# Windowed attention with sink keys, then a gated two-layer product: adjacent score blocks, a third bank in the first product, and constant products on TensorE in the first group

## The chip, the core and the metric

The kernel runs on one core of a Trainium2 chip. A core has five engines with instruction queues of their own: TensorE (PE, matrix products and transposes, weight loads shown apart as PEld), VectorE (DVE), ScalarE (ACT), GpSimd (POOL) and SyncE (SP, which issues DMAs here). PE writes to PSUM, which has eight banks of 2 KB in each of 128 partitions; DVE and ACT read PSUM, POOL and the DMA engines do not. The metric is the device time of one execution in microseconds, as the median of several runs.

## The reference

Inputs are `q`, `k`, `v` of shape (4, 8, 768, 64), and two weight matrices of 512 x 2048 and 2048 x 512.

```python
scores = scale * np.matmul(q, k.transpose(0, 1, 3, 2))
keep = is_sink | in_window                  # 4 first keys, or the last 128
scores = np.where(keep, scores, -1000000000.0)
scores = scores - np.max(scores, axis=-1, keepdims=True)
a = np.exp(scores)
a = a / (np.sum(a, axis=-1, keepdims=True) + 1e-09)
attn = np.matmul(a, v)
x = attn.transpose(0, 2, 1, 3).reshape(B * S, H * D)      # 3072 x 512
h = x @ w_in
g = h * (1.0 / (1.0 + np.exp(-1.702 * h)))
out = g @ w_out
```

## The kernel before

The 3072 rows are cut into 12 groups of 256 (`g`, 0 to 11), three for each batch entry. A group goes through attention, then the first product with its activation, then the second product, and three groups are in work at a time: in stage `n` PE does attention of group `n`, the first product of group `n - 1` and the second product of group `n - 2`. The whole order of instructions is written out by hand (`tc.manual_schedule()`), so each engine runs its instructions in the order in which the code issues them, and a wait on one engine holds up all that stands behind it on that engine.

Attention of a group is done for four pairs of heads (`hp`, 0 to 3):

- `qk_block` (L146) transposes q and k on PE into a PSUM tile `tqk`, which DVE or ACT copies to `qkT`. It is used for groups 0 to 3; from group 4 on a DMA transposes (`transposed_qk`, L167).
- `sinks` (L188) gives the four sink scores (`sk`) and, on DVE, their minimum.
- `scores` (L209) gives a pair of heads' scores: eight products of 64 rows each, into a tile `nat` of two banks. Products with `masked_l` and `masked_r`, two constant matrices of 128 x 128, stand in for the keys before the first row.
- `maxima` (L234) is DVE's work on `nat`: a predicated copy, a maximum over rows, and `bias`.
- `weights` (L249) is ACT's: four exponentials from `nat` to `A`.
- `weights_transposed` (L261) transposes `A` to `AT`, on PE and through a PSUM tile `tA` for groups 0 to 2, by DMA from group 3 on. POOL (`upper`, L311) and DVE (`lower`, L301) mask `AT`.
- `values` (L324) multiplies with `v` into a tile `av`, and `normal` (L355) divides on DVE into `xn`. `x_transposed` (L366) turns `xn` into `xT`, on PE for groups 0 and 1 (`tx`), then by DMA.

`hidden` (L384) is the first product, in eight tiles `hT` of two times 128 columns of `w_in`; each tile is 8 products of 128 x 256, and ACT's activation (L397) takes it to `gT`. `out_part` (L403) is a quarter of the second product for 128 rows: four products of 128 x 512 into the tile `o`. `out_store` (L431) copies `o` to `osb` (ACT for the first 128 rows, DVE for the second) and issues the store on SP.

PSUM is split by three tags. `mm` has two banks (`mm_bank`, L103) for `o` and `hT` and, in the first groups, for some of the transposes. `av` has two banks (`av_bank`, L106) for `sk`, `tAs`, `av` and the rest. `nat` has two tiles of two banks. A tile of a tag takes the place of the one two before it of the same tag, and its first product waits until that one has been read.

The order around the change:

- The first group: L479 to L484 transpose group 0's q and k as they land, L504 to L565 are the attention of groups 0 and 1, interleaved, with the loads of weights and later groups on POOL's queue in between. From L568 on `hidden(0, ...)` runs.
- `second` (L630) is the first half of stage `n` from 3 on: the weights of the first two pairs on ACT, the second product of group `n - 2` on PE, with `scores(n, 2)` (L640) between its two halves of 128 rows and `scores(n, 3)` (L648) after the first quarter of the second half. DVE's `maxima` follow each.
- The second half of the stage (L685 to L707) is `hidden(n - 1, F2)` for `F2` from 0 to 7, and between the tiles the sinks and the first two pairs' scores of group `n + 1` (`F2` = 1) and the values of group `n` (`F2` = 3, 4, 6, 7).

Of the kernel before, what the change touches and what calls it, by code (L numbers as in the profile page):

```python
# [10 lines left out]
FP32 = mybir.dt.float32  # L11
FP16 = mybir.dt.float16
# [5 lines left out]
P = 128  # L18
# [39 lines left out]
def kernel(  # L58
# [11 lines left out]
    nc = tc.nc  # L70
# [6 lines left out]
    NF = DF // P  # L77
    NT = S // TG
    NG = B * NT
# [6 lines left out]
    psp = ctx.enter_context(tc.tile_pool(name="psum", bufs=1, space=bass.MemoryType.PSUM))  # L86
# [19 lines left out]
    def av_bank(name, shape, dt=FP32):  # L106
        return psp.tile(list(shape), dt, tag="av", bufs=2, name=name)

    G = [dict() for _ in range(NG)]

    def load_part(g: int, part: int):


        b, t = divmod(g, NT)
        e, i = divmod(part, 2)
        rows = slice(t * TG + i * P, t * TG + (i + 1) * P)
        if part == 0:
            G[g]["qkn"] = work.tile([P, 4, DM], FP16, tag="qkn", bufs=3, name=f"qkn{g}")
        if part < 4:
            dst = G[g]["qkn"][:, part].rearrange("s (h d) -> s h d", h=H)  # L120
        else:
            dst = vn[b][t][:, i, :, 0:D]
        nc.gpsimd.dma_start(dst, (q, k, v)[e][b, :, rows].rearrange("h s d -> s h d"))  # L123
# [22 lines left out]
    def qk_block(g: int, a: int, eng):  # L146

        n, T = G[g]["qkn"], qk_tile(g)
        bank = mm_bank if g == 1 or (g, a // 2) == (0, 0) else av_bank
        tp = bank(f"tqk{g}_{a}", (P, HP, P), FP16)  # L150
        for c in range(HP):
            nc.tensor.transpose(tp[:, c], n[:, a, bass.ts(c, P)], ident)
        eng(out=T[:, bass.ts(a, HP)], in_=tp)  # L153
# [17 lines left out]
    def sink_keys(b: int, copy):  # L171
        kT = G[b * NT]["qkT"]
        for h in range(2):
            copy(
                out=kd[b][bass.ts(h, D), :, bass.ts(h, n_sink)],
                in_=kT[bass.ts(h, D), 1, 0, :, 0:n_sink],
            )

    def sink_values(b: int):
        nc.vector.tensor_tensor(  # L180
            out=vs[b][0:64, :, 0:D],
            in0=vsr[:, b].unsqueeze(1).broadcast_to((64, 16, D)),
            in1=sink_rows[0:64].unsqueeze(2).broadcast_to((64, 16, D)),
            op=ALU.mult,
        )
# [23 lines left out]
    def scores(g: int, hp: int):  # L209

        b, t = divmod(g, NT)
        qkT = G[g]["qkT"]
        nat = psp.tile([P, 2, 2, 2 * P], FP32, tag="nat", bufs=2, name=f"nat{g}_{hp}")
        for i in range(2):
            I = 2 * t + i
            prev = None if I == 0 else qkT[:, 1, 0, hp] if i else G[g - 1]["qkT"][:, 1, 1, hp]
            for part, keys in ((0, prev), (1, qkT[:, 1, i, hp])):
                for h in range(2):
                    r = bass.ts(h, D)
                    o = nat[:, h, i, bass.ts(part, P)]  # L220
                    if keys is None:
                        nc.tensor.matmul(o, masked_l[r], masked_r[r], start=True, stop=True)
                    else:
                        nc.tensor.matmul(o, qkT[r, 0, i, hp], keys[r], start=True, stop=True)  # L224
        G[g]["nat", hp] = nat
# [32 lines left out]
                )  # L258
        G[g]["A", hp] = A

    def weights_transposed(g: int, hp: int):  # L261
        A = G[g]["A", hp]
        AT = work.tile([P, 2, 2, P], FP16, tag="AT", bufs=6, name=f"AT{g}_{hp}")
        flat = AT.rearrange("p h i s -> p (h i) s")
        if g < 3:
            bank = av_bank if g == 2 or (g, hp) == (1, 3) else mm_bank
            tp = bank(f"tA{g}_{hp}", (P, 4, P), FP16)
            for a in range(4):
                nc.tensor.transpose(tp[:, a], A[:, a], ident)
            if g == 0 or hp < (2 if g == 2 else 3):  # L270
                nc.scalar.copy(flat, tp)
            else:
                nc.vector.tensor_copy(out=flat, in_=tp)
        else:
            nc.sync.dma_start_transpose(flat, A.rearrange("p a c -> p (a c)"))
        G[g]["AT", hp] = AT
# [89 lines left out]
    def x_transposed(g: int):  # L366
        xT = work.tile([P, 2 * HP, P], FP16, tag="xT", bufs=3, name=f"xT{g}")
        xn = G[g]["xn"].rearrange("p i a h d -> p (i a h d)")
        if g < 2:
            bank = mm_bank if g == 0 else av_bank  # L370
            for i in range(2):
                tp = bank(f"tx{g}_{i}", (P, HP, P), FP16)
                for c in range(HP):
                    nc.tensor.transpose(tp[:, c], xn[:, (HP * i + c) * P : (HP * i + c + 1) * P], ident)
                if g == 0 or i == 0:
                    nc.scalar.copy(xT[:, bass.ts(i, HP)], tp)
                else:
                    nc.vector.tensor_copy(out=xT[:, bass.ts(i, HP)], in_=tp)
        else:
            nc.sync.dma_start_transpose(xT, xn)  # L380
        G[g]["xT"] = xT.rearrange("p (i c) s -> p i c s", i=2)


    def hidden(g: int, F2: int):  # L384
        xT = G[g]["xT"]
        if F2 == 0:
            G[g]["gT"] = work.tile([P, NF, TG], FP16, tag="gT", bufs=3, name=f"gT{g}")

        bank = av_bank if g == NG - 2 and F2 in (2, 3) else mm_bank
        hT = bank(f"hT{g}_{F2}", (P, 2, 2, P))  # L390
        for f in range(2):
            F = 2 * F2 + f
            for c in range(4):
                nc.tensor.matmul(  # L394
                    hT[:, f], w_in16[:, c, bass.ts(F, P)], xT[:, :, c], start=(c == 0), stop=(c == 3)
                )
        nc.scalar.activation(  # L397
            out=G[g]["gT"][:, 2 * F2 : 2 * F2 + 2].rearrange("p f s -> p (f s)"),
            in_=hT.rearrange("p f i s -> p (f i s)"),
            func=AF.Gelu_apprx_sigmoid,  # L400
        )

    def out_part(g: int, i: int, part: int):  # L403

        if part == 0:
            G[g]["o", i] = mm_bank(f"o{g}_{i}")
        o, gT = G[g]["o", i], G[g]["gT"]
        for F in range(4 * part, 4 * part + 4):
            nc.tensor.matmul(o, gT[:, F, bass.ts(i, P)], w_out16[:, F], start=(F == 0), stop=(F == NF - 1))  # L409

    def out_last(g: int, i: int):
# [30 lines left out]
    ident = constant(nc.sync, "ident", np.eye(P, dtype=np.float16), FP16)  # L442
# [33 lines left out]
    load_w_in(3)  # L476
    for part in range(3):
        load_part(2, part)
    qk_block(0, 0, by_dve)  # L479
    qk_block(0, 1, by_act)  # L480
    sink_values(0)
    qk_block(0, 2, by_dve)
    qk_block(0, 3, by_act)
    sink_keys(0, nc.vector.tensor_copy)  # L484

    def ahead(n: int, hp: int):

        if n < NG:
            if hp == 0:
                sinks(n)  # L490
            scores(n, hp)
            maxima(n, hp)

    def o(g: int, i: int, *parts):
        if 0 <= g < NG:
            for p in parts:
                out_part(g, i, p)

    def valued(g: int, hp: int):
        values(g, hp)  # L500
# [5 lines left out]
    qk_block(1, 0, by_act)  # L506
    weights(0, 0)
    qk_block(1, 1, by_act)
    scores(0, 2)
    maxima(0, 2)  # L510
    weights(0, 1)
    qk_block(1, 2, by_act)
    qk_block(1, 3, by_act)
    scores(0, 3)
    maxima(0, 3)
    sink_terms(0)
# [3 lines left out]
    weights_transposed(0, 1)  # L520
    upper(0, 1)
    load_part(2, 3)
    ahead(1, 0)
    weights(0, 3)
    weights_transposed(0, 2)
    upper(0, 2)
    sink_weights(0)
    lower(0, 0)
# [8 lines left out]
    lower(0, 2)  # L537
    lower(0, 3)
    weights(1, 0)
    weights_transposed(1, 0)  # L540
    scores(1, 2)
    valued(0, 0)
    valued(0, 1)
    weights(1, 1)
    weights_transposed(1, 1)
    upper(1, 0)
    maxima(1, 2)
    scores(1, 3)
# [81 lines left out]
    def second(n: int, g2: int, att: bool):  # L630

        if att and n + 1 < NG and (n + 1) % NT == 0:
            sink_keys((n + 1) // NT, nc.gpsimd.tensor_copy)
        if att:
            for hp in (0, 1):
                weights(n, hp)
                weights_transposed(n, hp)
        o(g2, 0, 0, 1, 2, 3)
        if att:
            scores(n, 2)  # L640
            maxima(n, 2)
        if g2 == NG - 1:
            out_store(g2, 0)
            out_last(g2, 1)
            return
        o(g2, 1, 0)
        if att:
            scores(n, 3)  # L648
            maxima(n, 3)
            sink_terms(n)  # L650
        o(g2, 1, 1, 2, 3)
        out_store(g2, 0)
        if att:
            weights(n, 2)
            weights_transposed(n, 2)
        out_store(g2, 1)
        if att:
            weights(n, 3)
            weights_transposed(n, 3)
            sink_weights(n)  # L660
            lower(n, 0)
            if n + 2 < NG:
                transposed_qk(n + 2)
# [82 lines left out]
```

## Time and profile before

| | |
|---|---|
| three runs, median | 242.43 us |
| lowest, highest | 241.89, 242.43 us |
| the profiled execution | 242.06 us |
| its span, first to last instruction | 240.3 us |
| mean granted TensorE clock over the span, as recorded | 0.993 |
| chain of waits that ended last: PE, DMA, DVE, ACT | 64%, 16%, 7%, 5% |
| `hT` products (L394): 768, mean | 275 ns |
| `o` products (L409): 368, mean | 380 ns |
| activation of one `hT` tile (L397, ACT): mean | 597 ns |
| predicated copy and maximum of one `nat` tile (L236, L240, DVE): mean | 693 and 691 ns |

The busy time of a matrix product in this profile runs from its start to the modelled end of its result, so that products one after another overlap: a group of several shows the time from its first start to its last end. How fast PE really goes is read from the distance between starts. The granted clock is recorded from the first change on.

### The profile page before, as it was taken

What the parts mean: (1) busy time and instruction counts of PE and PEld (TensorE: products, weight loads), DVE (VectorE), ACT (ScalarE), POOL (GpSimd) and SP (SyncE); (2) the same over time, 40 slices, a digit from 0 to 9 for tenths busy, and PEclk for the clock granted to TensorE, in tenths of its full rate; (3) what the DMA queues carried; (4) which work ended last, traced back from release to release, by engine and by line L of the source; (5) the groups of instructions that cost most, each with busy time, mean ns of one, the idle gap of its engine ahead of it and who ended that gap; (6) DMA issues with size and microseconds to landing.
All of it is one profiled execution on the core that took longest, in us unless ns stands there. A gap on an engine that the chain in (4) does not pass through costs nothing.

```text
span 240.3 us, 5810 instructions
## 1 busy us (share of the span) xinstructions
PE 222.3 (93%) x2220; PEld 155.6 (65%) x2220; DVE 147.3 (61%) x388; ACT 156.7 (65%) x356; POOL 103.5 (43%) x158
## 2 busy tenths in 40 slices
PE   1677799999999999999999999999999999999994
PEld 0454578569569469478487486585585685684863
DVE  4787947579478377477675585776692883840100
ACT  2297774884875775785776777667668658760531
POOL 8988484857237357257046057148020310310000
PEclk9999989999999999999999999999999999999999
DMA  9999999999999969989989999999982513503102
GB/s 81 148 193 193 176 207 178 154 142 148 115 154 193 137 157 172 134 158 160 151 142 153 156 165 133 172 138 125 138 196 54 148 21 65 152 5 87 46 0 87
DMA packets 130699, 32.07 MB, mean 133 GB/s; under 512 B 123120, under 2 KB 127728, under 8 KB 130672
## 3 DMA queue, kind: packets, MB, share of 16 engines
q0 software_dynamic: 79104, 13.64, 79.2%
q1 hardware_dynamic: 50992, 17.88, 41.3%
q8 instruction: 17, 0.28, 0.5%
q10 hardware_dynamic: 576, 0.20, 0.3%
q14 instruction: 10, 0.08, 0.1%
HBM read 27.50 MB, written 6.29 MB: 141 GB/s over the span
## 4 chain that ended last, share of the span: by engine, by line
PE 64%; DMA 16%; DVE 7%; ACT 5%; POOL 4%; issue 2%; SPq 1%; ACTq 0%; DVEq 0%; POOLq 0%
PE hT L394 28%; PE o L409 25%; DMA qkn<-in_k_dram 5%; DMA AT<-A 4%; DMA qkT<-qkn 4%; DMA w_in<-in_moe_w_in_dram 3%; POOL qkn L123 3%; DVE m L240 3%; DVE nat L236 3%; PE nat L224 2%; PE av L344 2%; ACT L397 2%; PE av L332 2%; PE av L340 2%; PE o L420 1%
## 5 line engine op out<-in xcount | busy, mean ns | idle before, releaser
L394 PE MATMUL hT<-xT,w_in 128*128 128x256 f16 x768 | 95.6, 275 | 1.4 <-ACT gT L397 0.9
L409 PE MATMUL o<-w_out,gT 128*128 128x512 f16 x368 | 85.3, 380 | 0.0
L397 ACT ACTIVATE gT<-hT 128x512 f16<-128x512 f32 x96 | 56.2, 597 | 41.2 <-PE hT L394 40.9
L394 PEld LDWEIGHTS <-w_in 128*128 128x128 f16 x768 | 72.8, 98 | 13.7 <-issue 1.1
L318 POOL TENSOR_SCALAR_AFFINE_SELECT up<-AT 128x512 f16<-128x512 f16 (+1 forms) x48 | 27.2, 574 | 93.6 <-DMA AT<-A 86.0
L255 ACT ACTIVATE A<-nat,bias 128x128 f16<-128x128 f32 x192 | 53.7, 375 | 18.9 <-DVE bias L244 17.3
L409 PEld LDWEIGHTS <-gT 128*128 128x128 f16 x368 | 33.6, 98 | 37.2
L236 DVE COPY_PREDICATED nat<-prev,nat 128x512 f32<-128x512 uint16 x48 | 33.3, 693 | 28.0 <-PE nat L224 17.9
L240 DVE TENSOR_REDUCE m<-nat 128x4 f32<-128x512 f32 x48 | 33.2, 691 | 1.6
L123 POOL DMA_DIRECT2D vn<-in_v_dram x24 | 21.3, 895 | 5.3 <-DMA w_out<-in_moe_w_out_dram 4.0
L123 POOL DMA_DIRECT2D qkn<-in_q_dram x24 | 21.6, 908 | 1.4 <-POOLq L727 0.8
L123 POOL DMA_DIRECT2D qkn<-in_k_dram x24 | 21.3, 893 | 2.2 <-DMA w_in<-in_moe_w_in_dram 1.7
L362 DVE TENSOR_TENSOR xn<-av,rcp 128x256 f16<-128x256 f32 x48 | 20.4, 425 | 1.7
L305 DVE TENSOR_TENSOR lo<-AT,own 128x512 f16<-128x512 f16 (+1 forms) x48 | 18.7, 412 | 2.3 <-DMA AT<-A 2.3
L340 PE MATMUL av<-vn,up 128*128 128x65 f16 x160 | 18.3, 195 | 0.0
L344 PE MATMUL av<-vn,lo 128*128 128x65 f16 x160 | 18.3, 196 | 0.0
L361 DVE RECIPROCAL rcp<-av 128x4 f32<-128x4 f32 x48 | 8.6, 179 | 14.6 <-PE av L344 14.5
L332 PE MATMUL av<-vs,AsT 128*128 128x130 f16 x80 | 16.5, 224 | 0.5 <-DVE qkT L153 0.3
L224 PEld LDWEIGHTS <-qkT 64*128 64x128 f16 x352 | 11.7, 100 | 7.4 <-issue 6.6
L224 PE MATMUL nat<-qkT 64*128 64x128 f16 x288 | 16.5, 232 | 0.0
L340 PEld LDWEIGHTS <-up 128*128 128x128 f16 x160 | 14.8, 100 | 1.2 <-issue 0.4
L397 ACT ACT_TABLE_LOAD x11 | 14.1, 1283 | 0.2
(58 smaller groups left out, 179.3 us busy)
## 6 DMA issues: line engine op xcount, KB each, us to landing
out_dram<-osb SPq DMA_DIRECT2D x23, 256.0 KB
qkn<-in_q_dram POOLq DMA_DIRECT2D x24, 128.0 KB, 5.6
qkn<-in_k_dram POOLq DMA_DIRECT2D x24, 128.0 KB, 5.5
vn<-in_v_dram POOLq DMA_DIRECT2D x24, 128.0 KB, 6.2
w_in<-in_moe_w_in_dram POOLq DMA_DIRECT2D x4, 512.0 KB, 9.9
w_out<-in_moe_w_out_dram POOLq DMA_DIRECT2D x4, 512.0 KB, 12.4
AT<-A SPq DMA_TRANSPOSE x36
xT<-xn SPq DMA_TRANSPOSE x10
```

The costliest lines, as they stand in the source:

```text
L123: nc.gpsimd.dma_start(dst, (q, k, v)[e][b, :, rows].rearrange("h s d -> s h d"))
L224: nc.tensor.matmul(o, qkT[r, 0, i, hp], keys[r], start=True, stop=True)
L236: nc.vector.copy_predicated(out=nat[:, :, :, P:], mask=kinds(take_prev, g % NT), data=nat[:, :, :, 0:P])
L240: nc.vector.tensor_reduce(out=m1.rearrange("p h i -> p (h i)"), in_=nat.rearrange("p h i c -> p (h i) c")[:, :, P:], axis=AX.X, op=ALU.max,)
L255: nc.scalar.activation(out=A[:, 2 * h + i], in_=nat[:, h, i, P:], func=AF.Exp, bias=bias[:, i, hp, h : h + 1], scale=scale,)
L318: nc.gpsimd.affine_select(out=out, in_=in_, pattern=[[0, rows], [-1, P]], compare_op=ALU.is_gt, fill=zero_reg, base=0, channel_multiplier=1,)
L332: nc.tensor.matmul(av[:, i].rearrange("p h d -> p (h d)"), AsT, vs[b][:, c : c + 2].rearrange("p h d -> p (h d)"), start=True, stop=False,)
L340: nc.tensor.matmul(av[:, i, h], up[:, h, i], vn[b][J // 2][:, J % 2, head], start=False, stop=False)
L344: nc.tensor.matmul(av[:, i, h], own_w[:, h, i], vn[b][t][:, i, head], start=(I == 0), stop=(I == 0 or h == 1))
L394: nc.tensor.matmul(hT[:, f], w_in16[:, c, bass.ts(F, P)], xT[:, :, c], start=(c == 0), stop=(c == 3))
L397: nc.scalar.activation(out=G[g]["gT"][:, 2 * F2 : 2 * F2 + 2].rearrange("p f s -> p (f s)"), in_=hT.rearrange("p f i s -> p (f i s)"), fun ...
L409: nc.tensor.matmul(o, gT[:, F, bass.ts(i, P)], w_out16[:, F], start=(F == 0), stop=(F == NF - 1))
```

## The change

Three things are changed.

`second` now issues two products of the second half (`out_part(g2, 1, 0, 2)`), then `scores(n, 2)` and `scores(n, 3)` one right after the other, then both `maxima`, then the remaining fourteen products. `out_part` takes a range of products for this in place of a quarter.

`hidden` takes a bank of tag `av` in place of `mm` for the tile `F2` = 2 of groups 2 to 9. For group 10 it took one for `F2` = 2 and 3 before, and still does.

A new function `busy(n, out)` issues `n` products on PE whose result nothing reads: products of `masked_l` and `masked_r`, or, where `out` is of 16 bits, transposes of the identity. It is called thirteen times in the first two groups, for 151 products in all: 34 before the first transposes, 12, 7, 6 and 3 after each of group 0's `qk_block`, 24 and 8 ahead of `scores(0, 2)` and `scores(0, 3)`, 6 ahead of `scores(1, 0)`, 14 ahead of `scores(1, 1)`, 16 and 6 ahead of the transposes of `A` in `weights_transposed(1, 0)` and `(1, 1)`, and 10 and 5 within the first tile of `x_transposed(0)`. They write to a tile `warm0` of tag `nat`, a tile `warm1` of tag `av`, or to the place that the transpose after them writes.

```diff
+    def busy(n: int, out):
+        for _ in range(n):
+            if out.dtype == FP16:
+                nc.tensor.transpose(out, ident, ident)
+            else:
+                nc.tensor.matmul(out, masked_l, masked_r, start=True, stop=True)
...
-    def weights_transposed(g: int, hp: int):
+    def weights_transposed(g: int, hp: int, n_busy: int = 0):
...
             tp = bank(f"tA{g}_{hp}", (P, 4, P), FP16)
+            busy(n_busy, tp[:, 0])
...
                 for c in range(HP):
+                    if g == 0 and i == 0 and c > 1:
+                        busy((10, 5)[c - 2], tp[:, c])
                     nc.tensor.transpose(tp[:, c], xn[...], ident)
...
-        bank = av_bank if g == NG - 2 and F2 in (2, 3) else mm_bank
+        more = (2,) if 2 <= g < NG - 2 else (2, 3) if g == NG - 2 else ()
+        bank = av_bank if F2 in more else mm_bank
...
-    def out_part(g: int, i: int, part: int):
+    def out_part(g: int, i: int, F0: int, F1: int):
...
-        for F in range(4 * part, 4 * part + 4):
+        for F in range(F0, F1):
...
+    warm = psp.tile([P, 2, 2, 2 * P], FP32, tag="nat", bufs=2, name="warm0")[:, 0, 0, 0:P]
+    busy(34, warm)
     qk_block(0, 0, by_dve)
+    busy(12, warm)
     qk_block(0, 1, by_act)
+    busy(7, warm)
     sink_values(0)
     qk_block(0, 2, by_dve)
+    busy(6, warm)
     qk_block(0, 3, by_act)
+    busy(3, warm)
...
     qk_block(1, 1, by_act)
+    warm = av_bank("warm1", (P, P))
+    busy(24, warm)
     scores(0, 2)
...
     qk_block(1, 3, by_act)
+    busy(8, warm)
     scores(0, 3)
...
-    ahead(1, 0)
+    sinks(1)
+    busy(6, warm)
+    scores(1, 0)
+    maxima(1, 0)
     weights(0, 3)
     weights_transposed(0, 2)
+    busy(14, warm)
...
-    weights_transposed(1, 0)
+    weights_transposed(1, 0, 16)
...
-    weights_transposed(1, 1)
+    weights_transposed(1, 1, 6)
...
         o(g2, 0, 0, 1, 2, 3)
-        if att:
-            scores(n, 2)
-            maxima(n, 2)
...
-        o(g2, 1, 0)
+        out_part(g2, 1, 0, 2)
         if att:
+            scores(n, 2)
             scores(n, 3)
+            maxima(n, 2)
             maxima(n, 3)
             sink_terms(n)
-        o(g2, 1, 1, 2, 3)
+        out_part(g2, 1, 2, NF)
```

## The prediction

> **What bounds the kernel now.** I read four views in this order: the page, the busy time by stretch (cut where the granted clock changes), PE's timeline in the first group and in one later stage, and DVE's and ACT's timeline in that stage.
>
> The page:
>
> ```profile
> PE 222.3 (93%) x2220; PEld 155.6 (65%) x2220; DVE 147.3 (61%) x388; ACT 156.7 (65%) x356; POOL 103.5 (43%) x158
> ...
> PEclk9999989999999999999999999999999999999999
> ```
>
> PE is the bound, and its digits are 9 from slice 7 on. The first 30 us are different. Stretches of 3.41 us (columns: length, PE busy and instructions, granted clock, DMA share, GB/s):
>
> ```profile
> 15.24:18.65 3.41, 2.57 (x34) 1.00 1.37 199
> ...
> 22.06:25.48 3.42, 3.42 (x50) 1.00 1.36 199
> 25.48:28.89 3.41, 1.72 (x19) 1.00 2.27 163
> 28.89:32.30 3.41, 3.41 (x22) 0.50 1.28 205
> 32.30:35.71 3.41, 3.12 (x42) 1.00 1.24 208
> ```
>
> The granted clock is given as 1.00 before 28.89, but the spacing of the same eight transposes says otherwise (start, busy, what, count, idle before):
>
> ```profile
> 10.83 1.03 PE L152 MATMUL tqk<-ident,qkn 128*128 128x128 f16 x8
> 13.36 0.29 PE L222 MATMUL nat<-maskedr,maskedl 64*128 64x128 f16 x2 [1.49 <-ACT A L255]
> ...
> 44.05 0.61 PE L152 MATMUL tqk<-ident,qkn 128*128 128x128 f16 x8
> ```
>
> Less the length of the last one (0.31 us early, 0.22 late), seven spacings take 0.72 and 0.39 us: 0.103 against 0.056 us. So PE runs at half speed until about 25.5 us (the records of the clock begin there), at full speed for one stretch, at half again until 32.30, then at full speed to the end. A stretch with PE 100% busy was followed by full clock, one at 75% (15.24) was not, one at 50% (25.48) lost it, one at 91% (32.30) kept it.
>
> A stage of the steady part, group 6 (PE, then DVE, then ACT):
>
> ```profile
> 113.14 3.62 PE L409 MATMUL o<-w_out,gT 128*128 128x512 f16 x16
> 116.69 0.23 PE L222 MATMUL nat<-maskedr,maskedl 64*128 64x128 f16 x2
> ...
> 117.02 1.04 PE L409 MATMUL o<-w_out,gT 128*128 128x512 f16 x4
> 117.99 0.23 PE L222 MATMUL nat<-maskedr,maskedl 64*128 64x128 f16 x2
> ...
> 118.32 2.76 PE L409 MATMUL o<-w_out,gT 128*128 128x512 f16 x12
> 120.92 1.98 PE L394 MATMUL hT<-xT,w_in 128*128 128x256 f16 x16
> ...
> 123.36 0.33 PE L224 MATMUL nat<-qkT 64*128 64x128 f16 x6
> 123.76 1.47 PE L394 MATMUL hT<-xT,w_in 128*128 128x256 f16 x12
> ...
> 117.20 0.69 DVE L236 COPY_PREDICATED nat<-prev,nat 128x512 f32<-128x512 uint16 x1 [2.08 <-PE nat L224]
> ...
> 121.12 0.69 DVE L437 COPY osb<-o 128x512 f32<-128x512 f32 x1 [0.51 <-PE o L409]
> ...
> 123.12 1.08 ACT L397 ACTIVATE gT<-hT 128x512 f16<-128x512 f32 x2
> ```
>
> Here PE has no long idle time; what it loses are small steps around the scores and before `hT`.
>
> **The change part by part.** The order on DVE, ACT, POOL and SP, DMA issues included, is the same; only PE's order changes.
>
> *Adjacent scores (stages 3 to 11, nine of them).* Sixteen `o` products at 0.2155 us end at 113.14 + 3.45 = 116.59; the scores start at 116.69. Their eight products run in pairs, 8 x 128 / 2 / 2.4 GHz = 0.21 us, to 116.90; `o` resumes at 117.02. So a visit to 64-row products costs 0.10 us going in and 0.12 coming out, and two blocks with nothing between them pay once (as the pair for the next group, x2 and x6 twice up to 123.36, already does). Gross: 9 x 0.22 = 1.96 us.
>
> It also makes the first block later: two `o` products (0.43 us) now stand ahead of it, so DVE starts its two maxima at 117.64 instead of 117.20. What is queued behind them on DVE is the copy of the second `o` tile (L437), and the second `hT` tile takes that tile's bank. DVE needs 3.32 us from 117.20 to the end of `ts` (start 120.38 plus 0.14), so the copy starts at 120.96 and ends at 121.65, and `hT` 1 starts 0.05 later at 121.70. Before, it started at 121.86 (a constant 0.07 us of waiting, seen in every stage). So 0.16 to 0.17 of the 0.22 remains. In stages 3, 4, 5 and 10 the same DVE rows have an extra 0.18, 0.35, 0.31 and 0.37 us (mean 0.30), for which the trace names nothing; there `hT` 1 comes 0.13 later than now. Net: 5 x 0.17 - 4 x 0.13 = 0.33 us, with bounds of 1.96 (DVE never late) and -1.2 (late in all nine).
>
> *Third bank for the third tile of the first product.* Line 389's F2 = 2 tile waits for ACT to empty tile 0: the scores' last six products start at 123.36, so PE is free at about 123.62, and ACT ends tile 0 (0.60 of the 1.08 us) at 123.71; PE starts at 123.76. That wait is 0.14 to 0.15 in five stages, 0.09 in stage 3 and 0.50 in stages 4 and 10 (hT starts 89.20 and 192.73): 1.82 us. In an `av` bank the tile waits only for DVE's copy of `tAs`, done 0.4 us sooner. Next in line is tile 3, which then needs tile 0's bank: ACT's chain hangs on the maxima, so tile 0 is emptied at 123.71 + 0.44 = 124.15, while tile 3 is due at 121.70 + 1.76 (rest of tile 1, `tAs`, sinks, scores) + 0.87 = 124.33. 0.18 us to spare; all 1.82 is kept. Without the third bank the adjacent scores would lose.
>
> From these 2.15 us I take 0.4 for stage 8, where PE already waits 0.40 us at 163.34 for DVE behind a DMA transpose landing at 162.35: coming sooner there is only waiting longer. Steady part: -1.75 us.
>
> *Constant products (151 of them, all in the first 28 us).* At full clock 151 x 0.056 = 8.5 us, laid into PE's waits. The first 34 take 34 x 0.107 = 3.64 us from DVE's fills of the operands (done at 1.2) to about 4.9, ahead of the first piece of q at 5.25, so they cost nothing even at half clock; they and the next twelve cover a whole 3.41 us stretch wherever it begins. Cover for the others: 24 x 0.056 = 1.34 in the 1.49 us before 13.36; 14 x 0.056 = 0.78 in the 0.85 before 18.93; 16 x 0.056 = 0.90 in the 0.84 before 21.02; 15 x 0.056 = 0.84 in 0.81 + 0.32 ahead of two `tx`.
>
> What full clock brings there: PE is not the bound, DVE and ACT are (ACT has no idle from 11.47 to 19.5), so only PE's hops between them count. The third and fourth `tqk`, sinks and first scores: DVE starts 0.33 sooner than 9.97. The scores and `tA` for which ACT waited 0.61 at 20.11: 0.22 each, 0.45. `tA`, scores and values for which DVE waited 0.84 at 23.21: 0.45. So `hT` 0 starts 1.23 sooner than 28.47. Then the stretch at 0.50: its third `hT` tile starts at 32.94 since PE itself is slow; ACT would free the bank at 32.15, so another 0.75. Sum 1.98. A cap: the second q piece of group 3 lands at 42.35 and its transposes start at 44.43, so beyond 2.08 us PE waits for the DMA. Bounds 0 and 2.08; I take 1.9, near the cap, since each hop is taken from a row of its own.
>
> The stretches from 5 to 28 us would be 55 to 70% busy by these counts, between the 50% that lost the clock and the 91% that kept it. That is the open point.
>
> Sum: 242.06 (the profiled execution; span 240.3 and 1.76 around it) - 1.75 - 1.9 = 238.4. That execution is 0.37 below the median of the runs (242.43), so I forecast 238.6.
>
> **The rivals.**
> A. The forecast, 238.6, its own range 237.4 to 240.0.
> B. The clock is granted early but lost again between 5 and 28 us, because those stretches stay too thin. For it: 50% was too little. Against it: at half clock the same products take twice as long, fill the stretch and win it back. It keeps about half of the 1.9 and some constants stand in the way: 239.7. A rule of the Trainium skill (TensorE: Matmul & The Clock Gate, Part 4: PE-mode transpose) says that transposes do not count as activity for the clock. By that rule the 37 constants of 151 that are transposes (16, 6, 10 and 5, all after 19 us) do nothing, the loss at 28.89 stays, and 0.75 us of the sum goes: 239.4. The rows do not decide it, as no stretch here holds transposes alone.
> C. DVE becomes the bound of the handover: its extra 0.30 in all nine stages makes adjacency -1.2; the third bank then brings 1.82 - 0.4 - 1.2 = 0.2, and with 1.9: 240.0.
> D. Slower: the constants stay at half clock, and each block overruns its wait in PE's order: 12 x 0.107 - 0.77 = 0.51, then 0.47, 0.41, 1.08 (24 in 1.49), 0.86 (8 with no wait), 0.38, 0.65, 0.87, 0.64 and 0.48, 6.35 us. DVE's and ACT's slack takes about half: 242.06 + 3.2 - 1.75 = 243.5. It decides if no full clock is granted before about 15 us. Against it: a 100% busy stretch got it.
> E. The transfers hide it: the load queue is never empty until 53 us and stage 8 waits for a transpose. If that wait swallows all gained before it, stages 9 to 11 alone remain: 241.6.
>
> **How the numbers follow.** Chances: A 0.44, B 0.21, C 0.12, D 0.11, E 0.12. A difference under 0.3% (0.73 us) can't be told from none here; E lies on that line and gives 0.09 to it and 0.03 to faster. So faster 0.80, within 0.09, slower 0.11. The range runs from 236.9 (both caps: 1.96 + 1.82 + 2.08 off 242.43 is 236.6) to 241.8, which leaves out D and a little of E and of the low end.
>
> **What would show it.** Right: clock records starting near 5 us with no 0.50 after; eight transposes at 10 us taking 0.6 us; `hT` 0 at about 26.5 to 27.3; one pair of scores per stage; no wait ahead of the third `hT` tile; the second one at most 0.2 us late. Wrong: a 0.50 stretch between 5 and 33 us (B, D), waits of over 0.3 us at the second `hT` tile in most stages (C), or `av` waits for DVE growing from stage 8 on (E).

## The result, and the profile after

The changed kernel takes 240.50 us (median of 7 runs, 239.17 to 242.17) against 242.40 us (241.89 to 242.54): a ratio of 0.9912, 95% interval 0.9887 to 0.9938, 1.9 us faster. The forecast was 238.6 us, 3.8 us faster: 240.50 lies in the stated range (236.9 to 241.8), and outside the forecast's own (237.4 to 240.0). The profiled execution took 241.43 us, its span is 239.7 us. It is one of the slower ones of seven that spread over 3.0 us; the runs of the kernel before spread over 0.65 us beside them, and over 1.75 to 2.8 us on the three chips further down.

The page of the changed kernel, the lines that answer to those of before:

```profile
PE 225.9 (94%) x2371; PEld 161.4 (67%) x2371; DVE 147.6 (62%) x388; ACT 156.1 (65%) x356; POOL 104.2 (43%) x158
...
PEclk9999999999999999999999999999999999999999
```

The dip of the clock is gone. The first group on PE in the changed kernel (start, busy, what, count, idle before):

```profile
13.34 0.62 PE L161 MATMUL tqk<-ident,qkn 128*128 128x128 f16 x8
...
27.22 1.03 PE L408 MATMUL hT<-xT,w_in 128*128 128x256 f16 x8
...
30.94 1.03 PE L408 MATMUL hT<-xT,w_in 128*128 128x256 f16 x8 [0.19 <-ACT gT L411]
```

Eight transposes now take 0.62 us at 13 us into the span (1.03 before): full clock. The first `hT` tile starts at 27.22 in place of 28.47, the third at 30.94 in place of 32.94.

What PE waits for in the changed kernel (engine, line, for whom: us in total, times, longest):

```profile
PE hT L408 <- DVE osb L451: 2.7, 4, 1.0
...
PE hT L408 <- DMA xT<-xn: 0.9, 1, 0.9
```

Neither line was there before. Where the first comes from is seen in stage 4, PE first; the second is taken up behind the experiments.

```profile
80.53 0.23 PE L233 MATMUL nat<-qkT,qkT 64*128 64x128 f16 x2
...
81.09 3.20 PE L423 MATMUL o<-w_out,gT 128*128 128x512 f16 x14
84.12 1.04 PE L408 MATMUL hT<-xT,w_in 128*128 128x256 f16 x8
86.17 0.60 PE L408 MATMUL hT<-xT,w_in 128*128 128x256 f16 x4 [1.01 <-DVE osb L451]
```

DVE in the same stage, and POOL's maskings beside it (one line, two instructions):

```profile
82.94 0.70 DVE L245 COPY_PREDICATED nat<-prev,nat 128x512 f32<-128x512 uint16 x1 [0.28 <-issue]
83.67 0.69 DVE L249 TENSOR_REDUCE m<-nat 128x4 f32<-128x512 f32 x1
84.39 0.47 DVE L253 SCALAR_TENSOR_TENSOR bias<-m,m 128x4 f32<-128x4 f32 x1
84.90 0.61 DVE L291 TENSOR_TENSOR ts<-bias,sn 128x64 f32<-128x64 f32 x1
85.44 0.68 DVE L451 COPY osb<-o 128x512 f32<-128x512 f32 x1
...
84.22 1.22 POOL L328 TENSOR_SCALAR_AFFINE_SELECT up<-AT 128x512 f16<-128x512 f16 x2 [4.44 <-DMA AT<-A]
```

PE is through the first `hT` tile's products at 84.99 and then stands until 86.17, because the copy of `o` on DVE ends at 86.12. `bias` takes 0.47 us and `ts` 0.61, where 0.16 and 0.23 are usual, and both run while POOL masks `AT`. (`ts`, from `sink_terms`, combines `bias` with the sink scores; it is DVE's last operation ahead of the copy.)

From the distances between PE's starts, less the time that the columns need, the loss in stages 3 to 11 can be told apart. All in us, one profiled execution each (`e0` is the changed kernel again, the others are below):

| | before | changed | e0 | e3 bank alone | e4 adjacent alone | e6 POOL held | e7 no adjacency |
|---|---|---|---|---|---|---|---|
| time of this execution | 242.06 | 241.43 | 238.92 | 240.17 | 245.25 | 238.67 | 239.11 |
| stage 3 begins at | 61.45 | 60.03 | 60.02 | 60.86 | 60.79 | 59.98 | 60.11 |
| into and out of 64-row products | 5.46 | 3.50 | 3.50 | 5.45 | 3.50 | 3.50 | 5.46 |
| before `hT` 0 | 0.01 | 1.09 | 0.01 | 0.01 | 0.01 | 0.93 | 0.01 |
| before `hT` 1 | 0.65 | 4.07 | 2.41 | 0.66 | 3.46 | 1.38 | 1.03 |
| before `hT` 2 | 1.82 | 0.00 | 0.00 | 0.00 | 5.20 | 0.00 | 0.00 |
| before `av` | 0.44 | 0.37 | 0.64 | 0.89 | 0.03 | 0.54 | 0.23 |
| the last pair's `bias` and `ts` above 0.163 and 0.226 | 1.24 | 2.53 | 0.78 | 1.68 | 1.81 | 0.01 | 1.98 |
| length of stages 3 to 11 | 154.25 | 155.06 | 152.57 | 152.99 | 158.12 | 152.39 | 152.70 |

The switches lost 1.96 us and the third tile's wait 1.82, to the hundredth what was forecast. In this execution the wait before the second tile took 3.42 of it and a wait before the first tile 1.08, so that stages 3 to 11 became 0.8 us longer; in `e0` they became 1.7 us shorter. Some wait before the second tile is always there: 0.07 us a stage in the old order, 0.12 with adjacent scores.

### The profile page after: what moved, and what is told of

It is laid out like the page before. It is cut to its first block, busy times and chain, and to the rows that moved or that the text cites. A ratio compares the mean times of both kernels' runs of the same rounds, so it can differ in the third digit from the quotient of the medians.

```text
span 239.7 us, 6112 instructions
## 1 busy us (share of the span) xinstructions
PE 225.9 (94%) x2371; PEld 161.4 (67%) x2371; DVE 147.6 (62%) x388; ACT 156.1 (65%) x356; POOL 104.2 (43%) x158
## 4 chain that ended last, share of the span: by engine, by line
PE 70%; DVE 16%; DMA 8%; issue 3%; ACT 1%; POOL 0%; DVEq 0%; POOLq 0%
PE hT L408 31%; PE o L423 25%; DVE m L249 5%; DVE nat L245 5%; PE nat L233 4%; DMA xT<-xn 3%; DMA AT<-A 3%; PE av L354 2%; DMA qkn<-in_q_dram 2%; PE av L342 2%; PE av L350 2%; DVE bias L253 1%; PE o L434 1%; DVE xn L372 1%; DVE osb L451 1%
## 5 line engine op out<-in xcount | busy, mean ns | idle before, releaser
L423 PE MATMUL o<-w_out,gT 128*128 128x512 f16 x368 | 83.8, 379 | 0.0
L408 PEld LDWEIGHTS <-w_in 128*128 128x128 f16 x768 | 71.7, 98 | 17.1 <-issue 4.4
L411 ACT ACTIVATE gT<-hT 128x512 f16<-128x512 f32 x96 | 55.6, 597 | 37.2 <-PE hT L408 37.0
L328 POOL TENSOR_SCALAR_AFFINE_SELECT up<-AT 128x512 f16<-128x512 f16 (+1 forms) x48 | 27.7, 588 | 90.8 <-DMA AT<-A 83.5
L423 PEld LDWEIGHTS <-gT 128*128 128x128 f16 x368 | 34.3, 98 | 38.4
L350 PE MATMUL av<-vn,up 128*128 128x65 f16 x160 | 17.8, 192 | 0.0
L233 PE MATMUL nat<-qkT 64*128 64x128 f16 x288 | 13.9, 216 | 0.0
L233 PEld LDWEIGHTS <-qkT 64*128 64x128 f16 x352 | 10.8, 94 | 4.1 <-issue 3.3
```

Of the source, the lines that this page charges most:

```text
L328: nc.gpsimd.affine_select(out=out, in_=in_, pattern=[[0, rows], [-1, P]], compare_op=ALU.is_gt, fill=zero_reg, base=0, channel_multiplier=1,)
L350: nc.tensor.matmul(av[:, i, h], up[:, h, i], vn[b][J // 2][:, J % 2, head], start=False, stop=False)
L408: nc.tensor.matmul(hT[:, f], w_in16[:, c, bass.ts(F, P)], xT[:, :, c], start=(c == 0), stop=(c == 3))
L411: nc.scalar.activation(out=G[g]["gT"][:, 2 * F2 : 2 * F2 + 2].rearrange("p f s -> p (f s)"), in_=hT.rearrange("p f i s -> p (f i s)"), fun ...
```

## The experiments

The theory after the result: DVE's two small operations that read two operands from SBUF, `bias` and `ts`, are held up while POOL's masking of `AT` (`upper`, also from SBUF) runs; by making the maxima 0.43 us later the change put the end of DVE's row of work on top of that masking, and the copy of `o` behind it lets the second `hT` tile wait. Rivals: DVE's long rows come from something else that fell in the same time; or the earlier start moved the DMA transposes of later stages and so caused all of it.

Four kernels separate the parts, each set against the kernel before on one chip (242.66 us).

**e1_const**: the constants alone (diff against the changed kernel; `scores(n, 2)` and its maxima stand ahead of the second half again).

```diff
-        more = (2,) if 2 <= g < NG - 2 else (2, 3) if g == NG - 2 else ()
+        more = (2, 3) if g == NG - 2 else ()
...
-        out_part(g2, 1, 0, 2)
+        out_part(g2, 1, 0, 4)
         if att:
-            scores(n, 2)
```

> The kernel before with the 151 constant products alone (scores and banks as before). Theory (the start gained what the trace of the changed kernel shows, 1.4 us at the beginning of stage 3, and the loss lies in the later stages): 1.2 to 2.0 us faster than before, with one unbroken record of full clock from about 5 us. Rival (the early start only moves the loads and transposes of later stages into worse places, and that ate the gain): less than 0.6 us faster.

241.14 us, ratio 0.9953 (0.9927 to 0.9979): 1.5 us faster by the medians, in the theory's band, and 1.1 us by the ratio, just under it; above the rival's by both. Its profiled execution (243.16, the slowest of its twelve runs) shows why there is something in the rival:

```profile
PE hT L408 <- ACT gT L411: 1.8, 5, 0.5
...
PE hT L408 <- DMA xT<-xn: 0.8, 1, 0.8
```

Without adjacency the long `bias` and `ts` rows are there too (0.49 to 0.69 us in four of nine stages), and in the same four stages (4, 7, 8 and 10) PE waits 0.29 to 0.58 us for ACT before the third tile. Adjacency is not needed for a collision.

**e2_adj_bank**: adjacency and the third bank, no constants (against the changed kernel).

```diff
-        for _ in range(n):
+        for _ in range(0 * n):
...
-    warm = av_bank("warm1", (P, P))
```

> The changed kernel without the constant products. Theory (DVE's bias and ts, 0.43 us later, run beside POOL's masking of AT and are stretched; the second hT tile waits for DVE's copy behind them): between 0.7 us faster and 1.0 us slower than before, waits of 0.3 to 1.2 us at the second hT tile in most stages. Rival (the stretch came with the earlier start): 1.75 us faster, as predicted for this part, and waits under 0.2 us at the second hT tile.

241.25 us, 0.9940 (0.9918 to 0.9961), 1.4 us faster: between the two bands. PE waits for DVE's copy of `o` four times, 1.3 us (2.61 us before `hT` 1 by the distances), so the new wait needs no early start; but it is smaller than in the first profile of the changed kernel, and near that of `e0` (2.41).

**e3_bank**: the third bank alone (against the kernel before).

```diff
-        bank = av_bank if g == NG - 2 and F2 in (2, 3) else mm_bank
+        more = (2,) if 2 <= g < NG - 2 else (2, 3) if g == NG - 2 else ()
+        bank = av_bank if F2 in more else mm_bank
```

> The kernel before with the third bank alone. Theory (nothing on DVE is later, so the wait ahead of the third hT tile goes and nothing takes its place): 1.0 to 1.8 us faster, and no wait over 0.15 us at the second or third hT tile. Rival (the bank taken from the values' tag costs what it brings, or another wait appears behind it): within 0.4 us of before.

240.33 us, 0.9914 (0.9880 to 0.9948). The bank alone is as fast as the whole change: 2.3 us faster by the medians, above the theory's band, though the interval (1.3 to 2.9 us) covers most of it. Its waits before the second and third `hT` tile are 0.66 (as before) and 0.00 us in all; 0.45 us more goes before `av`.

**e4_adj**: adjacent scores alone (against the kernel before; `scores(n, 2)` and its maxima move here from ahead of the second half).

```diff
+        out_part(g2, 1, 0, 2)
         if att:
+            scores(n, 2)
             scores(n, 3)
+            maxima(n, 2)
             maxima(n, 3)
```

> The kernel before with adjacent scores alone (the third hT tile keeps its mm bank). Theory: the 0.22 us a stage are won on PE and lost at the second hT tile (DVE's copy late) and at the third (ACT's first activation 0.43 us later): 0.5 to 3 us slower than before. Rival (the order of scores does not matter beyond PE's own switch): 0.3 to 2 us faster.

245.47 us, 1.0121 (1.0091 to 1.0150): 2.8 us slower. PE's waits:

```profile
PE hT L408 <- ACT gT L411: 4.7, 8, 0.7
PE hT L408 <- DVE osb L451: 2.1, 4, 0.8
```

Both waits that the prediction worked out are there: the second tile for DVE's copy, and the third for ACT's first activation, which hangs on the same maxima. The 1.96 us on the switches are won and 6.2 us are lost.

The second four ran on another chip (before: 242.82 us), with the changed kernel among them.

**e0_after**: the changed kernel.

> The changed kernel itself, on the same chip as the next three, so that they can be set against it: 0.986 to 0.995 of before in every theory.

240.10 us, 0.9905 (0.9873 to 0.9936).

**e5_late_ts**: `ts` behind the copy of `o`.

```diff
             maxima(n, 3)
-            sink_terms(n)
...
         out_store(g2, 1)
         if att:
+            sink_terms(n)
             weights(n, 3)
```

> The changed kernel with the sink terms (ts) computed after DVE's copy of the second o tile and not ahead of it. Theory (what DVE still has to do between the second maximum and the copy sets the second hT tile): 0.5 to 1.8 us faster than the changed kernel, since 0.14 to 0.55 us a stage leaves that path. Rival (the second hT tile waits for something else than DVE's row of work): within 0.4 us of the changed kernel.

238.68 us, 0.9837 (0.9811 to 0.9863), 1.4 us faster than the changed kernel. The wait before the second `hT` tile is down to 0.75 us. What DVE does ahead of that copy sets the tile.

**e6_paced**: POOL's first two maskings held until `ts` is there.

```diff
             if n > 2:
+                nc.gpsimd.tensor_copy(out=pace, in_=G[n]["ts"][0:1, 0, 0:1])
                 upper(n, 0)
                 upper(n, 1)
```

> The changed kernel with a one-element copy on POOL ahead of its first two maskings of AT, which reads ts, so that these two never run beside DVE's bias and ts. No work of DVE, ACT or PE is moved. Theory (POOL's masking beside them stretches bias and ts): bias and ts of the last pair back at 0.16 and 0.23 us in all stages, waits at the second hT tile under 0.15 us, 0.8 to 2.2 us faster than the changed kernel, and its runs closer together. Rival (the stretch only falls in the same time; something else on DVE or in its instruction stream makes it): the long bias and ts rows stay, and the time is that of the changed kernel or up to 0.5 us longer.

238.54 us, 0.9820 (0.9797 to 0.9844), 1.6 us faster than the changed kernel, and its five runs lie within 1 us (237.86 to 238.81; the six of `e0` within 2.9). Stage 4 again, DVE and then POOL:

```profile
84.34 0.16 DVE L253 SCALAR_TENSOR_TENSOR bias<-m,m 128x4 f32<-128x4 f32 x1
84.54 0.23 DVE L291 TENSOR_TENSOR ts<-bias,sn 128x64 f32<-128x64 f32 x1
84.68 0.68 DVE L451 COPY osb<-o 128x512 f32<-128x512 f32 x1
...
84.90 0.17 POOL L701 COPY pace<-ts 1x1 f32<-1x1 f32 x1 [5.48 <-DVE ts L291]
85.03 1.40 POOL L328 TENSOR_SCALAR_AFFINE_SELECT up<-AT 128x512 f16<-128x512 f16 x2
```

Nothing was taken from DVE, and from the start of `bias` (84.34) to that of the copy it needs 0.34 us in place of 1.05 in the first profile of the changed kernel. In all nine stages the last pair's `bias` takes 0.162 to 0.165 us and `ts` 0.225 to 0.227. Over those nine stages the two are 0.01 us above their usual length, against 2.53 us in the changed kernel's first profile and 0.78 in `e0`. The rival of a mere coincidence falls. One part of the expectation missed: the wait before the second tile is not under 0.15 us everywhere. 0.19 us are left in stage 11 and 0.48 in stage 4, where DVE has 0.28 us of idle time "issue" ahead of its second predicated copy. That idle time is there in all fourteen profiles (0.27 to 0.28 us) and stays without a cause.

**e7_const_bank**: constants and bank, scores in their old places (against the changed kernel; `scores(n, 2)` and its maxima stand ahead of the second half again).

```diff
-        out_part(g2, 1, 0, 2)
+        out_part(g2, 1, 0, 4)
         if att:
-            scores(n, 2)
             scores(n, 3)
-            maxima(n, 2)
             maxima(n, 3)
```

> The changed kernel with the scores in their old places (constants and third bank alone). Theory (adjacency costs more on DVE's side than it saves on PE; the other two parts add up): 2.5 to 3.5 us faster than before and 0.7 to 1.6 us faster than the changed kernel. Rival (constants and bank do not add up, the earlier start being taken by DMA waits in later stages): 1.5 to 2.3 us faster than before, as the bank alone.

239.31 us, 0.9875 (0.9842 to 0.9908), 3.5 us faster than before by the medians. The changed kernel without adjacency is 0.8 us faster by the medians than with it, though the intervals overlap (0.9873 to 0.9936). Alone, the two parts gave 1.5 and 2.3 us by the medians, so they nearly add up, and the theory's bands hold. The profile shows why the old order does better: `bias` and `ts` of the last pair are 1.98 us too long here as well, but DVE stands idle for 0.51 us ahead of the copy of `o` where nothing is stretched, and this swallows most of it (1.03 us before the second tile, of which 0.65 are always there). With adjacent scores DVE has no idle time ahead of that copy, in any stage of the profiles of the changed kernel, `e2`, `e4` and `e6`.

Four more hold POOL back, on a third chip (before: 242.59 us).

**e8_one_paced**: as e6, with one product ahead of the scores.

```diff
-        out_part(g2, 1, 0, 2)
+        out_part(g2, 1, 0, 1)
...
-        out_part(g2, 1, 2, NF)
+        out_part(g2, 1, 1, NF)
```

> The changed kernel with POOL's maskings held behind ts (as in e6) and one product of the second half ahead of the scores in place of two. Theory (DVE's start sets the second hT tile): DVE starts 0.22 us sooner in each of nine stages, which matters only where its row is still late; 0 to 1.0 us faster than e6 (0.978 to 0.983 of before). Rival (the fourth pair's scores then wait for ACT to empty their tile, PE pays it): 0.3 to 1.0 us slower than e6.

238.97 us, 0.9834 (0.9797 to 0.9872): not told from e6, which ran on the other chip (0.9820), so that the ratios are compared here and below. Both mechanisms show in the profile: the wait before the second tile is down to 0.66 us from 1.38, and the fourth pair's scores wait for ACT, 0.10 us in each of stages 4, 7 and 10. This execution, the slowest of six, lost 1.75 us before the first `hT` tile of stage 6.

**e9_bank_const_paced**: e6 with the scores in their old places.

> Constants and third bank, scores in their old places, POOL's maskings held behind ts. With e6 it prices adjacency where POOL does not stretch DVE. Theory (adjacent scores are worth about the predicted 0.17 us in each of nine stages once the collision is gone): 0.8 to 1.6 us slower than e6, about 0.986 to 0.989 of before. Rival (adjacency is worth nothing, e6 gained by the holding alone): as fast as e6, 0.980 to 0.984.

239.18 us, 0.9843 (0.9814 to 0.9871). Against e6's 0.9820 (0.9797 to 0.9844) adjacency is worth 0.5 us or so with the collision gone, with intervals that overlap: between the two theories, and not settled by the times. The profiles say more. In stages 3, 6, 9 and 10, where neither of the two shows another wait, a stage takes 16.69 us (in stage 10, 17.15) here and 16.52 (16.98) in e6: 0.17 us less with adjacent scores, as forecast. In the other stages of e6's profile waits before `av`, before a first tile and before the second tile take it back.

**e10_before_paced**: the kernel before, POOL held.

```diff
+                nc.gpsimd.tensor_copy(out=pace, in_=G[n]["ts"][0:1, 0, 0:1])
                 upper(n, 0)
```

> The kernel before with nothing but POOL's maskings held behind ts. Theory (in the kernel before the same collision fell in about four of nine stages and cost a wait at the third hT tile in two of them): 0.3 to 1.2 us faster than before. Rival (the collision is peculiar to the changed order): within 0.3 us of before; or slower, if the maskings held back now delay the values.

242.47 us, 0.9991 (0.9968 to 1.0014): no difference, the rival is right. The long rows of `bias` and `ts` are gone here too (1.24 us over nine stages in the profile of before), and it brings nothing: the waits are 1.52 us before the third tile in place of 1.82, and 1.03 before `av` in place of 0.44. In the old order the copy of `o` has time to spare. What the stretch did cost, 0.36 us before the third tile of stage 10, is gone, and in this profile the longer waits before `av` take it back. The hold moves POOL's loads in the same way in both kernels; that it brings nothing here speaks against the loads as the reason of e6's gain.

**e11_late_paced**: e5 and e6 together, POOL held behind the last `bias` (against e6, beside the edit of e5).

```diff
-                nc.gpsimd.tensor_copy(out=pace, in_=G[n]["ts"][0:1, 0, 0:1])
+                nc.gpsimd.tensor_copy(out=pace, in_=G[n]["bias"][0:1, 0, 3, 0:1])
```

> The changed kernel with ts after DVE's copy of the second o tile (as in e5) and POOL's maskings held behind the last bias. Theory (both take work off the row that sets the second hT tile, but ts may now be stretched in its new place, which only ACT's sink weights wait for): 0.2 us faster to 0.4 us slower than e6. Rival (ACT's chain through the sink weights to the first activation sets the stage): 0.5 us or more slower than e6.

238.67 us, 0.9828 (0.9797 to 0.9858): as e6, as expected. The best version of the study is e6, 1.8% under the kernel before; e5, e8, e9 and e11 cannot be told from it by their intervals.

## Why the prediction was right in its mechanisms and forecast twice the gain

*Switches of adjacent scores: right.* 1.96 us forecast, 5.46 - 3.50 = 1.96 measured.

*Third bank: right.* All 1.82 us of the wait are gone, the tile behind it takes none of them (under 0.1 us in all before the later tiles, as before), and e4 bears out the sentence that adjacency loses without it.

*DVE later by 0.43 us, with the copy of `o` and the second `hT` tile behind it: the right chain, mis-sized.* Forecast was a net of 0.33 us, a loss of 1.63 out of 1.96. The wait before the second tile rose by 3.42 us in the first profile (0.65 to 4.07), so that adjacency cost 1.46 us there, and by 1.76 in `e0`, close to the forecast. Where nothing is stretched, the 0.17 us a stage are there (`e9`). The step that failed is the sentence that DVE's extra 0.30 us had no cause in the trace, and that it would come in four stages of nine. It had one: in three of the four (3, 5 and 10) a row stood beside POOL's masking, which began at 68.62, 102.93 and 188.67 us. Stage 5 of the kernel before, DVE and POOL (one line, two maskings):

```profile
103.10 0.54 DVE L281 TENSOR_TENSOR ts<-bias,sn 128x64 f32<-128x64 f32 x1
...
102.34 1.22 POOL L318 TENSOR_SCALAR_AFFINE_SELECT up<-AT 128x512 f16<-128x512 f16 x2 [4.85 <-DMA AT<-A]
```

Stage 11, which the prediction does not list, has such a row too (`ts` 0.59 us); the extra of stage 4 is the idle time "issue" named under e6. An extra with such a cause is no fixed amount in fixed stages. Over the nine stages it is 0.71, 0.78, 1.81 and 2.53 us with adjacent scores (`e2`, `e0`, `e4` and the first profile), and 1.24, 1.60, 1.68 and 1.98 without (before, `e1`, `e3` and `e7`). So these eight profiles do not show that the later row met more maskings. What adjacency did is to use up the 0.51 us of idle time ahead of the copy, so that all of the stretch reaches PE: in stages 5, 7 and 8 of the first profile `bias` and `ts` are 0.86, 0.42 and 0.55 us too long, and the second tile waits 0.98, 0.54 and 0.67, the 0.12 of every stage included. That this profile had 2.53 us of it and `e0` 0.78 is chance, as far as the runs tell.

A rule of the Trainium skill (SBUF — State Buffer, Who interferes with whom) would have named it: a VectorE instruction with two inputs in SBUF contends with a GpSimd instruction that reads SBUF. The trace agrees: in all fourteen profiles `bias` outside a masking takes 0.167 us on average (550 rows, 0.162 for the shortest), beside one 0.315 (122 rows, up to 1.04); `ts` 0.225 against 0.405; the maximum, which reads PSUM, 0.691 in both.

*Rival C came nearest in time* (240.0 against 240.5), and its reason is there: DVE became the bound of the handover. Its number is in part luck: it keeps the 1.9 us of the start, of which 1.15 came, and its sign, waits of over 0.3 us in most stages, is seen in four stages of nine, in the first profile and in `e0`. Rival E's sign, waits before `av` growing from stage 8 on, is not seen: stage 8 has 0.24 us in the first profile and 0.07 in `e0`, in place of 0.40, and stages 9 to 11 have none.

*Stage 8 and the transposes: another place.* I took 0.4 us off for a wait before `av` at a DMA transpose. The `av` waits hardly changed (0.44 in all before, 0.37 in the first profile, 0.64 in `e0`). What came is a wait for the transpose of `xn`, in stage 6 of the changed kernel (the chain of waits there: start, length, what):

```profile
112.97 0.42 DVE xn L372
113.42 7.72 DMA xT<-xn
121.14 0.05 issue
121.19 0.83 PE hT L408 x6
```

In `e0` the same transpose took 4.85 us (112.27 to 117.12) and PE did not wait. A wait of 0.6 us or more before a first tile is in the profiles of e1, e2, e6 and e8 too, and not in the other nine. Which packets it queued behind was not tried; that it is part of the spread of the runs is likely, and not shown.

*Constants: the mechanism right, the sum too large.* Full clock came at 5.26 us and stayed, and the first and third `hT` tiles started 1.25 and 2.00 us sooner (1.23 and 1.98 forecast). But stage 3 begins only 1.42 us sooner: 0.15 us went to the second piece of q of group 3 (the cap that was named, 42.54 against 42.35 for its landing), and 0.26 to DVE, whose scores of group 2 kept a transpose waiting at 49.42; the other 0.17 us were not traced. And the profile of before was one draw: in the five profiles without constants (e2, e3, e4, e10 and before) stage 3 begins at 60.79 to 62.21, mean 61.44; in the nine with them at 59.79 to 61.39, mean 60.29. The difference, 1.15 us, lies near what e1 measured (1.1 by the ratio, 1.5 by the medians). The term was 1.9.

*Rivals B and D are out.* The stretches from 5 to 29 us kept the clock; in all nine profiles with constants the record of full clock begins between 4.29 and 7.16 us and is not broken before 235 us. Stretches of 3.41 us in the changed kernel (length, PE busy and count, granted clock, DMA share, GB/s):

```profile
1.84:5.26 3.42, 3.42 (x34) 1.00 1.22 116
5.26:8.67 3.41, 2.45 (x37) 1.00 2.17 144
...
18.91:22.32 3.41, 3.32 (x55) 1.00 1.66 190
...
25.74:29.15 3.41, 2.73 (x24) 1.00 2.21 165
```

By columns alone (512 columns counted as the 0.2155 us between two starts at full clock, 128 columns as 0.107 us at half, and 64-row products as running in pairs) they are 51 to 67% busy. The rule of the Trainium skill that full clock does not engage for transposes, since they do not count as busy in the same way (TensorE: Matmul & The Clock Gate, Part 4: PE-mode transpose), is not borne out by these rows: in 18.91 to 22.32 transposes are 2.67 of the 3.32 us and the clock stayed. By columns the rest is about 20% of that stretch, less than the 25 to 30% at which the clock was lost in other profiles. In e4 it was even granted after such a stretch:

```profile
13.37:16.78 3.41, 3.30 (x40) 1.00 1.25 196
16.78:20.20 3.42, 1.65 (x25) 1.00 1.77 184
20.20:23.61 3.41, 2.98 (x30) 0.50 1.28 201
```

Its records of the clock begin at 16.78 us with full speed; of the 3.30 us ahead, 2.07 are sixteen transposes. The profile lists them as `MATMUL` with `ident` as an operand and does not show whether the mode that the rule names is on.

*The sum.* Start 1.15 in place of 1.9, and stages 3 to 11 between 0.8 us longer and 1.7 us shorter in two profiles of the changed kernel, in place of 1.75 shorter: 240.5 where 238.6 was forecast.

## What to carry to other kernels

Before an instruction is moved on an engine that is not the bound, write down what ends last behind it and how many tenths of a microsecond it has to spare; here the copy of `o` had 0.51 us at best, 0.43 us of delay and 0.22 us of saving used it up, and from then on every stretched row on DVE was a wait of PE. Where a row of the profile is longer in some stages than in others, look at what runs beside it on the neighbouring engine before calling it noise: two operations of 0.2 us became 0.6 each, and one copy of a single element on POOL won back 1.6 us. Read such a row in more than one execution: its sum over nine stages was 0.7 us in one and 2.5 in another. Measure the parts of a change alone as well: here one of three parts was worth the whole.

## What the runs showed of the hardware

- DVE's operations with two operands in SBUF that start while a masking runs on POOL are mostly stretched, about until that masking ends: `ts` of 0.23 us up to 0.70, `bias` of 0.16 up to 0.64. In 60 of 77 rows of `bias` that started within a masking this is seen; the 19 that started ahead of one took 0.16 us. The two rows of over 1.0 us (e2 and e10) began beside POOL's issue of a load, with a masking right behind it; of 157 beside such an issue alone eight were longer, up to 0.63 us, which stays without a cause. Operations that read PSUM are not stretched (the maximum takes 0.690 to 0.692 us beside a masking).
- PE's clock is recorded from its first change on, and what stands ahead of it on the page is not measured: in the kernel before, 1.00 is given for 20 us in which starts of 128-column products lie 0.103 to 0.107 us apart, against 0.056 later. When full clock comes without help differs between executions: at 25.5 us and lost again at 28.9 (before), at 26.0 and kept (e3), at 16.8, lost at 20.2 and back at 30.4 (e4), and only at 33.5 (e10).
- By columns, stretches of 3.41 us at 25% (e2), 27% (e4) and 30% (before) lost full clock, and those at 41% (e3) and more kept it. At half clock 63% did not win it (before), nor 71 to 75% (e10); 77% did (e4).
- From the 128-row products of `o` to 64-row ones PE loses 0.096 us, and 0.12 on the way back, at full clock and in every stage, and two blocks of 64-row products with nothing between pay it once (5.46 to 3.50 us over nine stages).
